# Where a sliding window's mask is applied: selections on POOL, or small products added in PSUM

## The chip, the cores and the metric

The kernel runs on one core of a Trainium2 chip. A core has five engines that run their own instruction queues in order and meet through semaphores: PE (TensorE, the matrix products), DVE (VectorE), ACT (ScalarE), POOL (GpSimd) and SP (SyncE, which here issues nearly all DMAs). PE writes to PSUM alone; DVE and ACT read PSUM, POOL doesn't. The metric is the device time of one execution in microseconds, lower is better.

## The reference, cut to what matters

```
x = A_x                                            # [1, 2048, 512]
g = sigmoid((x * gate_w).sum(-1, keepdims=True))
a = x @ dft_hid_re.T ; b = x @ dft_hid_im.T
A = dft_seq_re @ a - dft_seq_im @ b                # Fourier mixing

qkv = (x @ wqkv) -> q, k, v of 32 heads, 16 wide   # attention
scores = q @ k.T * 16 ** -0.5
mask = (i - j >= 0) & (i - j < 256)                # a sliding window of 256
p = softmax(where(mask, scores, -1e9))
B = (p @ v) @ wo
out = g * A + (1 - g) * B
```

## The kernel before, in words

**Precision.** Most products are made of three: a number is split into a high part of the type float32r (`hi_of`, by ACT) and the rest (`lo_of`, line 104, by DVE or, with `pool`, by POOL), and high x high, high x low and low x high are added up.

**Attention** goes through 8 groups of 4 heads with 16 blocks of 128 positions each, 128 steps in all (the loop at line 942). A step n issues, for each of 4 heads:
- `s_head` (line 404): S = scores of block n's 128 queries against up to 384 keys (line 417). DVE adds the mask, a bf16 tile with 1e30 outside of the window, and takes the row minimum of the negated scores (line 420). Minima of four steps are gathered; `m_rows` and `m_turn` (lines 424 and 430) split them into two parts, turn them with a DVE transposition, write them to DRAM (`m_scr`) and read them back as two further rows of `ring[0]`, so that a later product subtracts the maximum by itself.
- `t_head` (line 465), for the step nine behind (k = n - 9): T = the scores transposed, 128 keys against up to 384 queries, less the maxima (line 475), of which ACT takes the exponential into the tile `pt` (line 476). S uses one half of PE's rows and T the other half, so that both can be in the array at once.

T has no mask. After the four heads of a step, `t_mask` (line 478), deferred by three ticks, has POOL set `pt` to zero in the first 128 columns where the query is ahead of the key, and in the last 128 columns where it is 256 or more behind it: two `affine_select` over 128 x 4 x 128 numbers (lines 482 and 486). In the last two blocks of a group the second is left out.

Every four steps `pv` (line 489) multiplies `pt` by the values, for a block of 512 queries: 88 products (fewer for the first block of a group) of 64 rows and 32 columns of weights, into two banks, one for each half of the keys. A half of 64 keys is taken with 320 columns from its own first, so that the 64 columns ahead of it and behind are never read; for the first key block of a group the ones ahead are read. ACT copies one bank, DVE adds the other (lines 507 and 508), and the result goes to DRAM, where the row of sums is taken out and inverted (`o_pack`, `l_in`, `l_inv`, `l_back`).

**Banks.** S, T and the two outputs of `pv` take turns in four PSUM banks (`ps_a`): an S waits for DVE to be done with the bank two S before, a T for ACT.

**Dense work** is a Python generator, `dense` (line 675): projections to q and k (`qk_proj`), then the Fourier part (`ab_group`, lines 360 to 389, which adds and subtracts four row blocks, and `c_block`, the products along the sequence). `fill` (line 922) takes a fixed number of its products for each step and puts them behind S and T on PE: 1.55 per head while projections last, 2.3 later. Each is a pair, one for each half of the rows.

**Order.** Everything but this is put in place by `defer(ticks, fn)`, a list of due times in ticks (line 83); `tick` is called once per dense product and with 0.7 per head. So a step is about nine ticks, and each engine's queue is the order in which these calls fall due. The input matrices are compared with each other on the way (`check_next`, `compare`), which is work of POOL and ACT.

Results are evicted by `collect` and `evict_split` (line 264): ACT copies, DVE adds the other bank, ACT takes the high part, and DVE or POOL the low one (`qk_evict`, line 281, asks POOL for k and DVE for q). `split_raw` (line 112) splits a loaded weight in two halves; `pool` says how many of its low parts go to POOL.

Of the kernel before, what the change touches and what calls it, by code (L numbers as in the profile page):

```python
# [8 lines left out]
F32 = mybir.dt.float32  # L9
F32R = mybir.dt.float32r  # L10
BF16 = mybir.dt.bfloat16
# [11 lines left out]
NH = 4  # L23
NB = S // P
WIN = 384
BIG = 1e30
SCALE = 0.25
LAG = 9
# [23 lines left out]
def fnet_window_mix(ctx: ExitStack, tc: tile.TileContext, xT, x, wqk, wv, wm, wx, cc, wo, gw, out):  # L52
# [45 lines left out]
    def f(ap):  # L98
        return ap.bitcast(F32)
# [42 lines left out]
    def pt_tile(shape, dt=F32):  # L142
        return at.tile(shape, dt, name="pt", tag="pt", bufs=NPT)

    mask = const.tile([P, WIN], BF16, name="mask")
    T = [const.tile([P, U_W], F32, name=f"t{j}") for j in range(4)]
    nc.gpsimd.memset(T[0], 0.0)
    ps = ps_a.tile([P, 512], F32, name="t", tag="st")
# [39 lines left out]
    for h in range(2):  # L188
        nc.gpsimd.memset(f(ring[1][64 * h + 32:64 * h + 64]), -1.0)

    nc.gpsimd.affine_select(mask, mask, pattern=[[1, WIN]], compare_op=OP.is_gt, fill=BIG,
                            base=0, channel_multiplier=-1)
    nc.gpsimd.affine_select(mask, mask, pattern=[[-1, WIN]], compare_op=OP.is_ge, fill=BIG,
                            base=256, channel_multiplier=1)
    vpad = [const.tile([P, 4, NH, 32], F32, name=f"vpad{b}") for b in range(3)]
    for t in vpad:
        nc.gpsimd.memset(t, 1.0)
# [49 lines left out]
        tick()  # L247

    def es_tile():
        return ev.tile([P, U_W], F32, name="es", bufs=3)  # L250

    def collect(pss, then, scale=1.0):
        t = pt_tile([P, 512]) if len(pss) == 1 else es_tile()[:, 0:512]
# [20 lines left out]
    def qk_evict(g, ss, i, pss):  # L274
        hl = ev.tile([P, 2, 512], F32R, name="hl", bufs=4)

        def done():
            ld(qk_scr[i][g][ss].rearrange("a h p d l s -> (a h p d) l s"), f(hl[:]))
            if i:
                have.add(("qk", g, ss))  # L280
        evict_split(pss, hl[:, 1 - i], hl[:, i], (-SCALE, 1.0)[i], done, i == 1)

    def qk_first(w):
        accs = [acc() for _ in range(2)]
# [75 lines left out]
    def ab_group(q, w, beside):  # L360
        x = [ev.tile([P, U_W], F32, name="ev") for _ in range(3)]
        E, O = slice(0, H + 1), slice(H, 2 * H + 1)
        to = [slice(0, H + 1), slice(H + 1, 2 * H + 2)]

        def t0():
            pass

        def t2():
            minus(x[0], T[0], T[2], False)
            defer(2, plus, T[0], T[0], T[2])  # L370

# [32 lines left out]
    def s_head(n, j):  # L404
        p, h = divmod(j, 2)
        jb = n % NB
        u, jj = divmod(n - LAG, 4)
        if u not in ML:
            ML[u] = at.tile([P, 16], F32, name="nm")
            if not (0 <= LAG + 4 * u and LAG + 4 * u + 4 <= NS * NB):  # L410
                nc.vector.memset(ML[u], 0.0)
        c = (h * 2 + p) * 4 + jj
        k0 = max(0, (jb - 2) * P)
        w = (jb + 1) * P - k0
        r = slice(64 * h, 64 * h + 48)
        ps = ps_a.tile([P, 512], F32, name="s", tag="st")
        nc.tensor.matmul(ps[:, :w], ring[0][r, p, jb * P:(jb + 1) * P], ring[1][r, p, k0:k0 + w],  # L417
                         start=True, stop=True)
        sm = at.tile([P, WIN], BF16, name="sm", bufs=1)
        nc.vector.tensor_tensor_reduce(out=sm[:, :w], in0=ps[:, :w], in1=mask[:, WIN - w:],  # L420
                                       scale=1.0, scalar=3e38, op0=OP.add, op1=OP.min,
                                       accum_out=ML[u][:, c:c + 1])

# [4 lines left out]
        defer(1, m_turn, u, m, hl)  # L428

    def m_turn(u, m, hl):  # L430
        nc.vector.tensor_sub(hl[:, 1], m, f(hl[:, 0]))  # L431
# [33 lines left out]
    def t_head(n, j):  # L465
        p, h = divmod(j, 2)
        kb = n % NB
        q0 = kb * P
        w = min(WIN, S - q0)
        if n not in PT:  # L470
            PT[n] = pt_tile([P, NH, WIN])
        pt = PT[n]
        r = slice(64 * h, 64 * h + 50)
        ps = ps_a.tile([P, 512], F32, name="t", tag="st")
        nc.tensor.matmul(ps[:, :w], ring[1][r, p, q0:q0 + P], ring[0][r, p, q0:q0 + w], start=True, stop=True)  # L475
        nc.scalar.activation(pt[:, j, :w], ps[:, :w], AF.Exp, scale=-1.0)  # L476

    def t_mask(n):
        w = min(WIN, S - n % NB * P)
        pt = PT[n]  # L480
        a = pt[:, :, 0:P]
        nc.gpsimd.affine_select(a, a, pattern=[[0, 4], [1, P]], compare_op=OP.is_ge, fill=0.0,  # L482
                                base=0, channel_multiplier=-1)
        if w == WIN:
            a = pt[:, :, 2 * P:3 * P]
            nc.gpsimd.affine_select(a, a, pattern=[[0, 4], [-1, P]], compare_op=OP.is_gt, fill=0.0,  # L486
                                    base=0, channel_multiplier=1)

    def pv(u, last=False):
        g, sb = divmod(u, 4)  # L490
# [2 lines left out]
        for kb in kbs:  # L493
            pt = PT[g * NB + kb]
            v2 = V2[g * 4 + kb // 4][:, kb % 4]
            for j in range(NH):
                for h in range(2):
                    r = slice(64 * h, 64 * h + 64)
                    a = max(kb * P + (64 * h if kb else 0), sb * 512)
                    e = min(kb * P + 64 * h + 320, sb * 512 + 512)  # L500
                    nc.tensor.matmul(ot[h][32 * j:32 * j + 32, a - sb * 512:e - sb * 512], v2[r, j],  # L501
                                     pt[r, j, a - kb * P:e - kb * P], start=kb == kbs[0], stop=kb == kbs[-1],
                                     skip_group_check=True)
# [4 lines left out]
        defer(3, lambda: nc.vector.tensor_add(os, ot[1], os))  # L508
        hf = g // 4
        us, ls = u_scr[sb][hf], l_scr[sb][hf]  # L510
        d = 14 if hf else 40

        def o_out():
            ld(us[g % 4].rearrange("j r s -> (j r) s"), os)
# [7 lines left out]
            defer(d, l_in)  # L522

        def l_in():
            lt = at.tile([P, 64], F32, name="lt", bufs=2)
            ld(lt, ls[0].rearrange("j (a b) -> (j a) b", b=64))
            defer(d, l_inv, lt)

# [146 lines left out]
    def dense():  # L675
# [9 lines left out]
        for ss in range(4):  # L685
            if ss:
                yield from qk_proj(0, ss, wq0)
            for c in range(4):
                if ss < 3 and c in (1, 2):
                    for a in range(2):  # L690
                        split_x(ss + 1, 2 * c - 2 + a, 1 + 4 * a)
                    if ss < 2:
                        defer(9, load_x, ss + 2, c - 1)
                if ss == 3 and c == 0:
                    raw = load_raw(wqk[1])
                if ss == 3 and c == 2:
                    w = split_raw(raw, 1, 3, 1)
                yield from v_proj(ss * 4 + c, wvs)
        for g in range(1, NG):
            for ss in range(4):  # L700
# [29 lines left out]
            if g < 3:  # L730
                for q in (2 * g - 2, 2 * g - 1):
# [5 lines left out]
                    if q % 2 == 0:  # L737
                        wraw[:] = [load_raw(wqk[g + 1])]
                    else:
                        nextw = split_raw(wraw[0], 1, 3, 1)  # L740
                    yield from ab_group(q, ws, beside)
                w = nextw
        have.add("proj")
# [198 lines left out]
    for n in range(N + LAG + 1):  # L942
# [4 lines left out]
        for p in range(NH):  # L947
# [163 lines left out]
```

## Time and profile before

| what | value |
| --- | --- |
| median of 3 runs | 736.88 us (731.63 to 739.27) |
| the profiled execution | 736.22 us |
| its span | 734.5 us |
| granted TensorE clock | 0.877 of full |
| busy PE / DVE / ACT / POOL | 605.2 / 485.2 / 430.0 / 438.6 us |
| chain that ended last | PE 42%, DMA 15%, DVE 14%, ACT 10%, POOL 7%, issue 7% |

The span is the profiler's, from the first instruction to the last. "Busy" is the time in which an engine has at least one record open; PE's records are pipelined, and their ends are modelled, so PE's busy time says more than its need. A row of the groups names line, engine and operation, output and inputs, shapes, how often, then the busy time in us, the mean length of one in ns, and the idle time just before them with what ended it. A row of waits reads "engine, tile, line <- what it waited for: us in total, times, longest". PEld is the loading of weights, SPq the queue of SP.

### The profile page before, as it was taken

How to read it: one execution, taken by the hardware profiler on the slowest of the kernel's cores; microseconds unless marked ns; L12 is line 12 of the kernel's file. 1: busy time of each engine (PE TensorE's matmuls, PEld its weight loads, DVE VectorE, ACT ScalarE, POOL GpSimd, SP SyncE). 2: the span in 40 equal slices, each digit the busy share in tenths (PEclk: the TensorE clock that was granted, in tenths of full speed). 3: DMA queues.
4: the chain of work that ended last, by engine and by line, in shares of the span. 5: the costliest groups of instructions: out<-in, count | busy, mean ns of one | idle time of the engine just before them, and what ended most of it. 6: DMA issues, size and time to landing. Idle time of an engine off the chain costs nothing.

```text
span 734.5 us, 17636 instructions
## 1 busy us (share of the span) xinstructions
PE 605.2 (82%) x6222; PEld 451.9 (62%) x6222; DVE 485.2 (66%) x1386; ACT 430.0 (59%) x985; POOL 438.6 (60%) x521
## 2 busy tenths in 40 slices
PE   9999799789788888998897778757778889559785
PEld 6788567555464765655565557646666666437554
DVE  5278676877787667787864666685577687344561
ACT  6344577667555667665564757656656777662220
POOL 6022565756676756579684887988997865320000
PEclk9999998999889899999987997767867899858899
DMA  7868777776564766875768778855737774655783
GB/s 287 278 210 239 224 203 223 221 231 201 146 207 135 224 189 209 254 218 167 212 204 268 244 226 280 262 146 192 214 89 211 238 183 124 186 172 152 241 275 129
DMA packets 93606, 152.62 MB, mean 208 GB/s; under 512 B 33028, under 2 KB 42116, under 8 KB 93380
## 3 DMA queue, kind: packets, MB, share of 16 engines
q1 hardware_dynamic: 92068, 149.28, 66.8%
q10 hardware_dynamic: 1440, 2.10, 0.8%
q8 instruction: 53, 0.87, 0.6%
q14 instruction: 45, 0.37, 0.2%
HBM read 108.56 MB, written 47.24 MB: 212 GB/s over the span
## 4 chain that ended last, share of the span: by engine, by line
PE 42%; DMA 15%; DVE 14%; ACT 10%; POOL 7%; issue 7%; SPq 3%; DVEq 0%; ACTq 0%; POOLq 0%
PE d L246 15%; PE o L501 8%; PE s L417 6%; DVE sm L420 6%; PE t L475 6%; PE d L242 4%; DMA ring<-m_scr 3%; DVE mhl L431 3%; SPq L96 3%; ACT pt L476 3%; DMA raw<-cc 3%; ACT cv L543 3%; PE t L242 2%; DMA big<-o_scr 2%; DVE es L508 2%
## 5 line engine op out<-in xcount | busy, mean ns | idle before, releaser
L420 DVE CUSTOM_DVE_ANT_0 sm<-s,mask 128x384 bf16<-128x384 f32 (+2 forms) x512 | 271.2, 530 | 105.1 <-PE s L417 56.8
L476 ACT ACTIVATE pt<-t 128x384 f32<-128x384 f32 (+2 forms) x512 | 231.2, 474 | 110.9 <-PE t L475 85.0
L475 PE MATMUL t<-ring,ring 50*128 50x384 f32 (+2 forms) x512 | 218.8, 442 | 61.9 <-ACT pt L476 23.3
L246 PE MATMUL d<-big,hl 64*128 64x512 f32 (+2 forms) x1440 | 254.0, 387 | 0.6 <-DVE es L257 0.6
L417 PE MATMUL s<-ring,ring 48*128 48x384 f32 (+2 forms) x512 | 200.3, 403 | 34.3 <-DVE nm L420 29.1
L246 PEld LDWEIGHTS d<-big,hl 64*128 64x128 f32 x1440 | 183.1, 225 | 6.5 <-issue 1.9
L482 POOL TENSOR_SCALAR_AFFINE_SELECT pt<-pt 128x512 f32<-128x512 f32 x128 | 85.7, 670 | 140.7 <-ACT pt L476 136.6
L417 PEld LDWEIGHTS s<-ring,ring 48*128 48x128 f32 x512 | 107.4, 214 | 101.0 <-DVE nm L420 86.8
L475 PEld LDWEIGHTS t<-ring,ring 50*128 50x128 f32 x512 | 108.7, 215 | 95.7 <-ACT pt L476 47.6
L246 PE MATMUL d<-hl,big 64*128 64x512 f32 x600 | 111.7, 416 | 0.0
L501 PE MATMUL o<-pt,vpad 64*32 64x320 f32 (+5 forms) x2816 | 88.2, 389 | 13.9 <-POOL pt L482 11.3
L501 PEld LDWEIGHTS o<-pt,vpad 64*32 64x32 f32 x2816 | 68.4, 116 | 36.1 <-POOL pt L482 13.8
L339 POOL TENSOR_TENSOR cv<-cv 128x256 f32<-128x256 f32 (+1 forms) x64 | 75.2, 1175 | 15.8 <-DMA cv<-cc 15.7
L486 POOL TENSOR_SCALAR_AFFINE_SELECT pt<-pt 128x512 f32<-128x512 f32 x112 | 75.8, 677 | 0.0
L246 PEld LDWEIGHTS d<-hl,big 64*128 64x128 f32 x600 | 66.8, 195 | 4.8 <-issue 1.0
L342 POOL TENSOR_TENSOR cv<-cv 128x512 f32<-128x512 f32 x48 | 63.1, 1315 | 8.9 <-DMA cv<-cc 8.9
L507 ACT COPY es<-o 128x512 f32<-128x512 f32 x32 | 18.7, 586 | 78.3 <-PE o L501 76.1
L543 ACT ACTIVATE cv<-cv 128x768 f32<-128x768 f32 x72 | 60.6, 842 | 0.6 <-POOL cv L339 0.6
L508 DVE TENSOR_TENSOR es<-o,es 128x512 f32<-128x512 f32 x32 | 22.1, 691 | 53.3 <-ACT es L507 38.3
L105 POOL TENSOR_TENSOR hl<-raw,hl 128x512 fp32r<-128x512 f32 x35 | 46.0, 1327 | 2.4 <-ACT hl L102 2.4
L242 PE MATMUL t<-big 128*128 128x512 f32 x144 | 39.6, 435 | 9.1 <-DVE fin L896 9.1
L105 POOL TENSOR_TENSOR hl<-es,hl 128x512 fp32r<-128x512 f32 x14 | 18.1, 1290 | 46.1 <-ACT hl L102 45.6
(98 smaller groups left out, 639.2 us busy)
## 6 DMA issues: line engine op xcount, KB each, us to landing
cv<-cc SPq DMA_DIRECT2D x64, 512.0 KB
qk_scr<-hl SPq DMA_DIRECT2D x32, 512.0 KB
ring<-qk_scr SPq DMA_DIRECT2D x128, 128.0 KB
ring<-qk_scr SPq DMA_DIRECT2D x128, 64.0 KB
u_scr<-es SPq DMA_DIRECT2D x32, 256.0 KB
raw<-cc SPq DMA_DIRECT2D x16, 512.0 KB
fin<-r_scr SPq DMA_DIRECT2D x17, 256.0 KB
big<-c_scr SPq DMA_DIRECT2D x16, 258.0 KB
```

What stands on the lines that cost most here:

```text
L105: (nc.gpsimd if pool else nc.vector).tensor_sub(lo, raw, f(hi))
L242: nc.tensor.matmul(pss[0], w, x, start=start, stop=stop, skip_group_check=skip)
L246: nc.tensor.matmul(pss[h], w[r], x[r], start=start, stop=stop, skip_group_check=skip)
L339: (nc.gpsimd if pool else nc.vector).tensor_sub(out, a, b)
L417: nc.tensor.matmul(ps[:, :w], ring[0][r, p, jb * P:(jb + 1) * P], ring[1][r, p, k0:k0 + w], start=True, stop=True)
L420: nc.vector.tensor_tensor_reduce(out=sm[:, :w], in0=ps[:, :w], in1=mask[:, WIN - w:], scale=1.0, scalar=3e38, op0=OP.add, op1=OP.min, accu ...
L475: nc.tensor.matmul(ps[:, :w], ring[1][r, p, q0:q0 + P], ring[0][r, p, q0:q0 + w], start=True, stop=True)
L476: nc.scalar.activation(pt[:, j, :w], ps[:, :w], AF.Exp, scale=-1.0)
L482: nc.gpsimd.affine_select(a, a, pattern=[[0, 4], [1, P]], compare_op=OP.is_ge, fill=0.0, base=0, channel_multiplier=-1)
L486: nc.gpsimd.affine_select(a, a, pattern=[[0, 4], [-1, P]], compare_op=OP.is_gt, fill=0.0, base=0, channel_multiplier=1)
L501: nc.tensor.matmul(ot[h][32 * j:32 * j + 32, a - sb * 512:e - sb * 512], v2[r, j], pt[r, j, a - kb * P:e - kb * P], start=kb == kbs[0], st ...
L543: nc.scalar.activation(junk, src, AF.Abs, accum_out=dst)
```

## The change

T is masked on its bank, ahead of the exponential. The mask is the one that DVE adds to S; its two triangles of 64 x 64 are copied at the start for each half of the rows into `edge`, and `unit` holds two identities. After T's product, two products per head of `unit` (64 x 64, bf16) with `edge` (64 rows, twice 64 columns, or 64 in the last two blocks) add 1e30 to the elements outside of the window: one for keys 0 to 63 and one for keys 64 to 127, into columns 0 to 127 and 256 to 383 in steps. The exponential then gives zero. `t_mask` goes. As the 64 columns ahead of the second half of keys aren't masked, `pv` no longer reads them in the first block either, and the addition there starts at column 64.

Some work is moved from DVE to POOL: the low part of the maxima in `m_turn` (the transposition follows two ticks later, in `m_out`), of q in `qk_evict`, of the second half of three weights (`split_raw` with 2), and two subtractions of `ab_group`. The tiles `es` are 512 columns instead of 516, `lt` has one buffer instead of two, and a delay ahead of `o_pack`, `l_in` and `l_inv` is 30 ticks instead of 40.

```diff
-    mask = const.tile([P, WIN], BF16, name="mask")
+    mask = const.tile([P, MASK_W], BF16, name="mask")
+    edge = const.tile([P, 2, 64], BF16, name="edge")
+    unit = const.tile([P, 64], BF16, name="unit")
...
+    for a in range(2):
+        r = slice(64 * a, 64 * a + 64)
+        for e in range(2):
+            c = 64 * a + 256 * e + 1
+            nc.gpsimd.tensor_copy(edge[r, e], mask[r, c:c + 64])
+    ones = ev.tile([P, U_W], F32, name="ev")[:, 0:P]
+    nc.gpsimd.memset(ones, 1.0)
+    for m in (1, -1):
+        nc.gpsimd.affine_select(ones, ones, pattern=[[m, P]], compare_op=OP.is_ge, fill=0.0,
+                                base=0, channel_multiplier=-m)
+    for a in range(2):
+        r = slice(64 * a, 64 * a + 64)
+        nc.gpsimd.tensor_copy(unit[r], ones[r, r])
...
-        evict_split(pss, hl[:, 1 - i], hl[:, i], (-SCALE, 1.0)[i], done, i == 1)
+        evict_split(pss, hl[:, 1 - i], hl[:, i], (-SCALE, 1.0)[i], done)
...
-            minus(x[0], T[0], T[2], False)
+            minus(x[0], T[0], T[2])
...
-            minus(T[2], T[1], T[3], False)
+            minus(T[2], T[1], T[3])
...
     def m_turn(u, m, hl):
-        nc.vector.tensor_sub(hl[:, 1], m, f(hl[:, 0]))
+        minus(hl[:, 1], m, f(hl[:, 0]))
+        defer(2, m_out, u, hl)
+
+    def m_out(u, hl):
         mt = at.tile([P, 32], F32, name="mt", bufs=1)
...
-        nc.tensor.matmul(ps[:, :w], ring[1][r, p, q0:q0 + P], ring[0][r, p, q0:q0 + w], start=True, stop=True)
+        nc.tensor.matmul(ps[:, :w], ring[1][r, p, q0:q0 + P], ring[0][r, p, q0:q0 + w], start=True, stop=False,
+                         skip_group_check=True)
+        ends = ps.rearrange("p (e c) -> p e c", e=2)
+        d = slice(64 * h, 64 * h + 64)
+        e = 2 if w == WIN else 1
+        for a in range(2):
+            o = slice(64 * a, 64 * a + 64)
+            nc.tensor.matmul(ends[o, 0:e, o], unit[d], edge[d, 0:e], start=False, stop=True, skip_group_check=True)
         nc.scalar.activation(pt[:, j, :w], ps[:, :w], AF.Exp, scale=-1.0)
-
-    def t_mask(n):
...
-                    a = max(kb * P + (64 * h if kb else 0), sb * 512)
+                    a = max(kb * P + 64 * h, sb * 512)
...
-        defer(3, lambda: nc.vector.tensor_add(os, ot[1], os))
+        c = slice(0 if sb else 64, 512)
+        defer(3, lambda: nc.vector.tensor_add(os[:, c], ot[1][:, c], os[:, c]))
...
-        d = 14 if hf else 40
+        d = 14 if hf else 30
...
-                    w = split_raw(raw, 1, 3, 1)
+                    w = split_raw(raw, 1, 3, 2)
...
-            if p == 3 and 0 <= k < N:
-                defer(3, t_mask, k)
```

More of the change, by code (lines that the diff above doesn't have):

```diff
@@ L25 @@
 WIN = 384
+MASK_W = 386
 BIG = 1e30
@@ L189, in fnet_window_mix @@
         nc.gpsimd.memset(f(ring[1][64 * h + 32:64 * h + 64]), -1.0)
-    nc.gpsimd.affine_select(mask, mask, pattern=[[1, WIN]], compare_op=OP.is_gt, fill=BIG,
+    nc.gpsimd.affine_select(mask, mask, pattern=[[1, MASK_W]], compare_op=OP.is_gt, fill=BIG,
                             base=0, channel_multiplier=-1)
-    nc.gpsimd.affine_select(mask, mask, pattern=[[-1, WIN]], compare_op=OP.is_ge, fill=BIG,
+    nc.gpsimd.affine_select(mask, mask, pattern=[[-1, MASK_W]], compare_op=OP.is_ge, fill=BIG,
                             base=256, channel_multiplier=1)
+    for a in range(2):
[11 more added lines that the diff above has]
+        nc.gpsimd.tensor_copy(unit[r], ones[r, r])
     vpad = [const.tile([P, 4, NH, 32], F32, name=f"vpad{b}") for b in range(3)]
@@ L249, in es_tile @@
     def es_tile():
-        return ev.tile([P, U_W], F32, name="es", bufs=3)
+        return ev.tile([P, D], F32, name="es", bufs=3)
     def collect(pss, then, scale=1.0):
@@ L419, in s_head @@
         sm = at.tile([P, WIN], BF16, name="sm", bufs=1)
-        nc.vector.tensor_tensor_reduce(out=sm[:, :w], in0=ps[:, :w], in1=mask[:, WIN - w:],
+        nc.vector.tensor_tensor_reduce(out=sm[:, :w], in0=ps[:, :w], in1=mask[:, WIN - w:WIN],
                                        scale=1.0, scalar=3e38, op0=OP.add, op1=OP.min,
@@ L474, in t_head @@
         ps = ps_a.tile([P, 512], F32, name="t", tag="st")
-        nc.tensor.matmul(ps[:, :w], ring[1][r, p, q0:q0 + P], ring[0][r, p, q0:q0 + w], start=True, stop=True)
-        nc.scalar.activation(pt[:, j, :w], ps[:, :w], AF.Exp, scale=-1.0)
-    def t_mask(n):
[L479 to L487, printed above, removed]
+        nc.tensor.matmul(ps[:, :w], ring[1][r, p, q0:q0 + P], ring[0][r, p, q0:q0 + w], start=True, stop=False,
[6 more added lines that the diff above has]
+            nc.tensor.matmul(ends[o, 0:e, o], unit[d], edge[d, 0:e], start=False, stop=True, skip_group_check=True)
+        nc.scalar.activation(pt[:, j, :w], ps[:, :w], AF.Exp, scale=-1.0)
     def pv(u, last=False):
@@ L524, in l_in @@
         def l_in():
-            lt = at.tile([P, 64], F32, name="lt", bufs=2)
+            lt = at.tile([P, 64], F32, name="lt", bufs=1)
             ld(lt, ls[0].rearrange("j (a b) -> (j a) b", b=64))
@@ L739, in dense @@
                     else:
-                        nextw = split_raw(wraw[0], 1, 3, 1)
+                        nextw = split_raw(wraw[0], 1, 3, 2)
                     yield from ab_group(q, ws, beside)
```

## The prediction

> **What bounds the kernel now.** I read the page first, then the stage in which T's products run (72 to 665 us), the waits inside it, and single switches of PE's tiles in the timeline. The page's chain, and the stage's row:
>
> ```profile
> PE d L246 15%; PE o L501 8%; PE s L417 6%; DVE sm L420 6%; PE t L475 6%; PE d L242 4%; DMA ring<-m_scr 3%; DVE mhl L431 3%; SPq L96 3%; ACT pt L476 3%; DMA raw<-cc 3%; ACT cv L543 3%; PE t L242 2%; DMA big<-o_scr 2%; DVE es L508 2%
> ```
>
> ```profile
> core 0: us, PE busy (x) PEld busy (x) DVE busy (x) ACT busy (x) POOL busy (x), PEclk, DMA share, GB/s
> 72.00:665.00 593.00, 482.92 (x5549) 355.79 (x5553) 412.13 (x1222) 384.04 (x898) 418.70 (x497) 0.86 0.68 203
> ```
>
> No engine fills the stage, and the chain passes through all of them. PE's 483 us count records that overlap: a record lasts longer than the array needs for it. These rows give PE's own need, the first from a stretch where only dense products run:
>
> ```profile
> 60.32 1.56 PE L246 MATMUL d<-big,hl 64*128 64x512 f32 x12
> ```
>
> ```profile
> L246 PE MATMUL d<-big,hl 64*128 64x512 f32 x576 | 130.5, 452 | 0.0
> L246 PE MATMUL d<-hl,big 64*128 64x512 f32 x431 | 89.9, 425 | 0.0
> L246 PE MATMUL d<-big,hl 64*128 64x258 f32 x576 | 80.6, 328 | 0.0
> L246 PE MATMUL d<-big,hl 64*128 64x256 f32 x192 | 33.3, 367 | 0.0
> ```
>
> ```profile
> 125.27 2.45 PE o L501 x63
> ```
>
> Twelve products (six pairs, one for each half of the rows) take 1.56 us with the last one's tail, about 0.23 us a pair. So the stage's 1007 long dense products need 503 x 0.23 = 116 us, the 768 half as long some 384 x 0.12 = 46, 32 blocks of o some 2.4 each = 77, and 512 pairs of s and t, which run beside each other, 0.17 each (shown below) = 87. Together 326 of 593 us. The rest is waiting, in these groups:
>
> ```profile
> PEld s L417 <- DVE nm L420: 86.8, 179, 4.6
> ...
> PEld t L475 <- ACT pt L476: 47.6, 55, 8.2
> ...
> PE s L417 <- DVE nm L420: 29.1, 41, 4.4
> PE t L475 <- ACT pt L476: 23.3, 26, 4.3
> PE t L475 <- DMA ring<-m_scr: 23.3, 9, 8.0
> ...
> PEld t L475 <- DVE es L508: 17.0, 28, 2.7
> PEld o L501 <- POOL pt L482: 13.8, 6, 5.2
> PEld t L475 <- issue: 13.5, 6, 5.2
> PE o L501 <- POOL pt L482: 11.3, 5, 4.9
> ```
>
> They add up to 266 us: s waits for its bank because DVE is behind (116 us, 220 times), t because ACT is (71 us, 81 times), o for POOL's selections (25 us). The kernel is bound by four engines that take turns in being late, with two banks' depth between them.
>
> **What goes.** POOL loses its selections, and DVE loses several operations to POOL:
>
> ```profile
> L482 POOL TENSOR_SCALAR_AFFINE_SELECT pt<-pt 128x512 f32<-128x512 f32 x128 | 85.7, 670 | 140.7 <-ACT pt L476 136.6 <-DMA cv<-cc 3.1 <-PE s L417 0.6
> L486 POOL TENSOR_SCALAR_AFFINE_SELECT pt<-pt 128x512 f32<-128x512 f32 x112 | 75.8, 677 | 0.0
> L431 DVE TENSOR_TENSOR mhl<-nm,mhl 128x16 fp32r<-128x16 f32 x33 | 40.2, 1219 | 3.8 <-ACT mhl L102 3.7
> L105 DVE TENSOR_TENSOR hl<-es,hl 128x512 fp32r<-128x512 f32 x14 | 13.8, 984 | 2.6 <-ACT hl L102 1.1 <-POOL hl L105 0.8 <-issue 0.6
> L105 POOL TENSOR_TENSOR hl<-es,hl 128x512 fp32r<-128x512 f32 x14 | 18.1, 1290 | 46.1 <-ACT hl L102 45.6
> ```
>
> POOL sheds 85.7 + 75.8 = 161 us and takes 14 low parts (18 us), 8 subtractions of ab_group (about as wide: 8 x 1.29 = 10), 3 halves of a weight split (4) and 33 small subtractions of the maxima. The last have no row on POOL; between 0.04 us (16 of 512 columns of the last row) and the 1.2 us that DVE took, 1 to 40 us, I take 0.3 each = 10, nearer to the first, since they are 16 columns wide. POOL ends near 419 - 161 + 42 = 300 us. DVE sheds 40 + 14 + 8 + 3 = 65 us. On the chain lie these three:
>
> ```profile
> 473.22 12.11 DVE mhl L431
> ...
> 544.07 5.95 DVE mhl L431
> ...
> 562.48 5.12 DVE mhl L431
> ```
>
> A subtraction of 16 columns takes 12.1 us there, while POOL's queue runs without a gap; 23 us are on the chain. Gone, I credit 20 of these 23 us, 20 of the 25 us in which o waits for POOL (the rest will be ACT's exponential), and 13 for the other low parts and subtractions: 53 us at most, and only where PE is still the one that waits.
>
> The Trainium skill (SBUF — State Buffer, Who interferes with whom) says that a VectorE instruction with two SBUF inputs contends with GpSimd's reads for a shared interface; the 12.1 us agree. By that rule the transposition, with one input, is never held so, and all of the 23 us would come off, 3 us more.
>
> The maxima come later by two ticks, about 1 us at 9 ticks a block, and the transposition on DVE now waits for POOL's subtraction. Behind it on DVE stand the next L420, and behind these s on PE. One POOL operation in flight costs up to 1.3 us, so 0 to 43 us in 33 turns against the 40 taken away; I take 5, because two ticks cover most of it and POOL's queue is shorter. What is late next would be t's read of m_scr, 23.3 us of waits now; a slower PE stretches ticks as well, so I leave that term alone. Masks and units are made by some ten small POOL instructions at the start, and POOL then waits for work and T for 72 us:
>
> ```profile
> 20.00:40.00 20.00, 20.00 (x101) 15.56 (x101) 5.82 (x18) 7.17 (x14) 0.00 (x0) 1.00 0.77 258
> ```
>
> That costs nothing. The earlier o_pack (30 ticks) and the single lt buffer move three SP transfers that nobody waits for before the tail: nothing; 64 columns less of o and es for the first block: under 3 us, not counted.
>
> **What comes.** Behind each of 512 t products stand two products of 64 x 64 weights and up to 128 columns, in another tile shape than t (64 x 128) before them and than s or d (64 x 128) behind. The trace has such changes of shape at o (64 x 32):
>
> ```profile
> 106.07 0.67 PE L246 MATMUL d<-big,hl 64*128 64x512 f32 x2
> 106.67 0.34 PE L501 MATMUL o<-pt,vpad 64*32 64x64 f32 x8
> ```
>
> ```profile
> 109.02 0.50 PE L246 MATMUL d<-big,hl 64*128 64x512 f32 x2
> 109.35 0.33 PE L475 MATMUL t<-ring,ring 50*128 50x384 f32 x1
> 109.36 0.28 PE L417 MATMUL s<-ring,ring 48*128 48x256 f32 x1
> 109.48 0.45 PE L246 MATMUL d<-big,hl 64*128 64x512 f32 x2
> ```
>
> ```profile
> 109.01 0.18 PEld L246 LDWEIGHTS d<-big,hl 64*128 64x128 f32 x2
> ```
>
> ```profile
> L246 PE MATMUL d<-hl,big x600: 383/393/770, 37.1 to 361.2; 64*128 64x512 f32 x150
> ```
>
> Into o: d's records end at 106.74 and o starts 0.07 us before that, instead of a pair's 0.23 after d's start; so it waits for the array to empty. Out of o: the weights of d are loaded only at 109.01, with d itself, whose record is 0.50 where the median is 0.39 (the second figure of the last row); the load, hidden elsewhere, shows with 0.11. Within one shape t and s start together, and the next d follows 0.13 to 0.17 us later.
>
> For one t then: its record is 0.33, so the small pair starts 0.26 after it. A product of 128 columns lasts 0.22 (t's 384 take 0.33, s's 256 take 0.28, so 128 columns are worth 0.05); weights that show add between nothing and the 0.11 of 128 columns, I take half, 0.06, for 64; the next shape starts 0.07 before the end, at 0.26 + 0.21 = 0.47, and streams after its own 0.11, at 0.58. That is 0.41 us more than 0.17: 512 x 0.41 = 210 us of PE's time. The bounds: 0.06 if the pair needs nothing but its 128 columns (31 us), 0.25 if the array empties but loads stay hidden (128), 0.50 if both loads show fully (256). I take 0.41, as o's switches show both parts each time.
>
> The Trainium skill (TensorEngine Tiling (Array Packing), Key Properties) says that changing the tiling mode, and not just the tile, drains TensorE, and lists 64 x 64 as a mode of its own; o's switch agrees, but no run here shows 64 x 64.
>
> **The sum.** PE's need in the stage goes from 326 to 536 of 593 us. Of the 210 us, what falls where PE waits anyway is free. The 220 waits for DVE, 81 for ACT, 28 for es and 26 others of the rows are 355, about 300 of the 512 cycles once those that coincide count once, and each hides at most 0.41: 120 us. So 90 remain. The waits left, 266 - 120 = 146 us, shrink by what was taken from DVE and POOL, 53, and grow by 5: 90 - 53 + 5 = +42 us on the profiled execution's own 736.2 us. That is 778; the exponentials' start 0.2 us later is inside the 0.41. Against this, a slower PE leaves DVE and ACT more time for each block than the count of waits shows, some 8 us: **770 us**. The profiled execution lies 0.7 us under the median of the runs, which changes nothing.
>
> **The rivals.** *Small products are free of switches* (not slower, in fact faster): where the pair costs 0.06 us, 31 us, half of it inside waits, and the 53 us come off: 736 + 15 - 53 = 698. For it: s, t and d of different row halves do start together (109.35 and 109.36). Against it: every o block. It decides at less than about 0.2 us a pair. Chance 0.22. The Trainium skill (TensorE: Matmul & The Clock Gate, Part 3: Packing small matmuls) lets weight loads overlap products of another row group, without a word on shapes; that is this rival's mechanism, and by it the time would be this rival's.
> *Emptied, but absorbed*: 0.25 us a pair, 128 us; the same 300 waits hide 75, and DVE's shorter queue is given to PE: 128 - 75 - 53 = 0: 736. For it: PE waits 266 us. Chance 0.18.
> *PE sets the pace and ACT lags*: 0.50 us a pair, 256 us, and only the 220 + 81 long waits hide 0.45 of it at best two times in three: 256 - 90 - 53 = +113, cut by the 30 us of waits that cannot recur: about 820. For it: PE is in order, and a late t holds s and d. Chance 0.10.
> Of the change not doing what it says I see no sign: the selections are gone from the program.
>
> **How the numbers follow.** Forecast 0.50, rivals 0.22, 0.18 and 0.10. A measurement of this kernel tells about 1% from no change. Slower by over 1%: 0.50 + 0.10 less a little of the first = 0.59; the middle case spreads on both sides: within 1% 0.12; faster 0.29. The range leaves out half of each far case: 698 to 818; the forecast's own is 748 to 795.
>
> **What would show it.** Right: the two small products start 0.2 us or more behind t, the next product's weights load only with it; exponentials wait longer for PE; no DVE operation of 5 us in the stage; POOL near 300 us; waits of s for DVE well under 116 us; PE busy over 90% of the stage. Wrong: the small pair starts inside t's record beside s or d, PE's share is unchanged, and the stage is shorter than 593 us; or the maxima's transposition waits for POOL by microseconds.

## The result, and the profile after

The changed kernel took 815.36 us (median of 4 runs, 809.81 to 834.97) beside 734.25 us (731.24 to 739.27) for the kernel before: 1.107 times as long, 95% interval 1.094 to 1.121. The profiled one of these four runs was a slow one (span 833.2 us, clock 0.817); the ratios leave such runs out, the medians don't, and the lines below are those of a repetition: span 820.1 us, clock 0.835, median of its two runs 822.8, ratio 1.118 (1.100 to 1.137).

From its page the span, the engines' busy times, the granted clock (in tenths of full, for each fortieth of the span), and the chain:

```profile
span 820.1 us, 19406 instructions
PE 763.9 (93%) x7246; PEld 487.9 (59%) x7246; DVE 422.8 (52%) x1328; ACT 439.7 (54%) x985; POOL 327.6 (40%) x348
PEclk9999699999759599999595879665959599667999
PE 66%; DMA 12%; POOL 7%; issue 5%; DVE 3%; ACT 3%; SPq 3%; POOLq 0%; DVEq 0%; ACTq 0%
PE d L262 31%; PE o L516 9%; PE t L501 9%; PE t L494 7%; PE s L433 5%; PE d L258 4%; SPq L97 3%; DMA ring<-qk_scr 3%; PE t L258 2%; DMA fin<-r_scr 2%; DMA big<-o_scr 2%; DMA ring<-m_scr 2%; DMA qk_scr<-hl 1%; POOL hl L106 1%; POOL t L358 1%
```

PE has gone from 42% of the chain to 66%, DVE from 14% to 3%, and the small products (`PE t L501`) alone hold 9%. The stage of T, which was 593 us long, is now 680; its columns are those of the row in the prediction:

```profile
72.00:752.00 680.00, 642.80 (x6581) 392.89 (x6586) 351.54 (x1172) 394.08 (x898) 300.31 (x311) 0.81 0.60 178
```

PE is busy in 642.80 of 680 us (95%, before 81%). POOL stands at 300.31, DVE fell from 412 to 351.54. Three of the page's groups, and of the waits of the whole execution those that matter:

```profile
L502 ACT ACTIVATE pt<-t 128x384 f32<-128x384 f32 (+2 forms) x512 | 236.6, 471 | 186.7 <-PE t L501 183.2
...
L433 PE MATMUL s<-ring,ring 48*128 48x384 f32 (+2 forms) x512 | 184.0, 368 | 2.0 <-DVE nm L436 1.7
...
L501 PEld LDWEIGHTS <-unit 64*64 64x64 bf16 x1024 | 57.5, 109 | 154.0 <-issue 152.5
```

```profile
DVE sm L436 <- PE s L433: 178.2, 305, 4.5
PEld L501 <- issue: 152.5, 498, 0.5
...
POOL mhl L355 <- ACT mhl L103: 95.4, 19, 21.9
...
DVE mt L452 <- POOL mhl L355: 32.1, 14, 7.4
```

The waits have turned round. S's products hardly wait for DVE any more (1.7 us, before 29.1); DVE waits for S (178.2 us, before 56.8) and ACT for the small products (183.2 us; for T before, 85.0). The row of `PEld L501` is the new one: 498 times the loading of the small weights stands 0.31 us on average, with nothing that the profile names to release it (it calls that "issue"). One such place in the timeline, first PE's products, then the weight loads:

```profile
199.94 0.34 PE L494 MATMUL t<-ring,ring 50*128 50x384 f32 x1
200.21 0.24 PE L501 MATMUL t<-edge,unit 64*64 64x128 bf16 x2
200.38 0.50 PE L262 MATMUL d<-hl,big 64*128 64x512 f32 x2
```

```profile
200.21 0.11 PEld L501 LDWEIGHTS <-unit 64*64 64x64 bf16 x2 [0.31 <-issue]
200.38 0.19 PEld L262 LDWEIGHTS d<-hl,big 64*128 64x128 f32 x2
```

The small pair starts 0.27 us behind T, 0.07 before the end of T's record, and its weights load only then; the next dense pair follows 0.17 later and its record is 0.50 instead of 0.39, with its own weights in the open. The Trainium skill (TensorEngine Tiling (Array Packing), Key Properties) says that a change of the tiling mode drains TensorE. This trace agrees for 64 x 64: the pair starts no earlier than 0.07 us before the end of T's record.

### The profile page after: what moved, and what is told of

Its sections match the earlier page's. It is cut to its first block, busy times and chain, and to the rows that moved or that the text cites. A ratio compares the mean times of both kernels' runs of the same rounds, so it can differ in the third digit from the quotient of the medians.

```text
span 833.2 us, 19406 instructions
## 1 busy us (share of the span) xinstructions
PE 778.2 (93%) x7246; PEld 495.3 (59%) x7246; DVE 423.5 (51%) x1328; ACT 439.9 (53%) x985; POOL 326.7 (39%) x348
## 4 chain that ended last, share of the span: by engine, by line
PE 63%; DMA 14%; POOL 7%; issue 5%; DVE 4%; ACT 3%; SPq 2%; DVEq 0%; POOLq 0%
PE d L262 30%; PE o L516 9%; PE t L501 8%; PE t L494 6%; PE s L433 4%; PE d L258 4%; DMA ring<-m_scr 3%; SPq L97 2%; DMA ring<-qk_scr 2%; DMA big<-o_scr 2%; PE t L258 2%; DVE es L524 1%; POOL hl L106 1%; POOL t L358 1%; POOL t L355 1%
## 5 line engine op out<-in xcount | busy, mean ns | idle before, releaser
L262 PE MATMUL d<-big,hl 64*128 64x512 f32 (+2 forms) x1440 | 264.6, 448 | 0.7 <-DVE es L273 0.7
L494 PE MATMUL t<-ring,ring 50*128 50x384 f32 (+2 forms) x512 | 206.6, 403 | 31.6 <-DVE es L524 13.9
L433 PE MATMUL s<-ring,ring 48*128 48x384 f32 (+2 forms) x512 | 187.4, 374 | 1.8 <-DVE nm L436 1.7
L262 PEld LDWEIGHTS d<-big,hl 64*128 64x128 f32 x1440 | 135.9, 223 | 33.2 <-issue 1.5
L501 PEld LDWEIGHTS <-unit 64*64 64x64 bf16 x1024 | 58.0, 110 | 158.6 <-issue 157.3
L501 PE MATMUL t<-edge,unit 64*64 64x128 bf16 (+1 forms) x1024 | 134.2, 259 | 0.0
L262 PE MATMUL d<-hl,big 64*128 64x512 f32 x600 | 124.9, 490 | 0.0
L516 PE MATMUL o<-pt,vpad 64*32 64x320 f32 (+4 forms) x2816 | 98.1, 429 | 1.1 <-ACT pt L502 0.8
L106 POOL TENSOR_TENSOR hl<-es,hl 128x512 fp32r<-128x512 f32 x28 | 36.4, 1300 | 124.9 <-ACT hl L103 124.2
L524 DVE TENSOR_TENSOR es<-o,es 128x512 f32<-128x512 f32 (+1 forms) x32 | 21.5, 671 | 83.5 <-ACT es L522 72.0
```

The costliest lines, as they stand in the source:

```text
L106: (nc.gpsimd if pool else nc.vector).tensor_sub(lo, raw, f(hi))
L262: nc.tensor.matmul(pss[h], w[r], x[r], start=start, stop=stop, skip_group_check=skip)
L501: nc.tensor.matmul(ends[o, 0:e, o], unit[d], edge[d, 0:e], start=False, stop=True, skip_group_check=True)
```

## The experiments

Four of them part the change into its pieces; the others follow what these left open. Ratios are to runs of the kernel before on the same chip; its medians were 734 to 741 us on the chips used, so differences between the medians of two experiments are good to some us only.

**1. The same masks in T's own shape.** The weights of the small products get 128 columns, an identity with zeros beside it, so that their tile is 64 x 128 like that of T, S and the dense products. The triangles are read straight from the mask.

```diff
-    unit = const.tile([P, 64], BF16, name="unit")
+    unit = const.tile([P, 192], BF16, name="unit")
...
-            nc.tensor.matmul(ends[o, 0:e, o], unit[d], edge[d, 0:e], start=False, stop=True, skip_group_check=True)
+            edge = mask[d, 64 * h + 1:64 * h + 321].rearrange("p (e c) -> p e c", c=64)[:, 0:4 * e - 3:4]
+            nc.tensor.matmul(ends[:, 0:e, o], unit[d, 64 - 64 * a:192 - 64 * a], edge, start=False, stop=True,
+                             skip_group_check=True)
```

> The changed kernel, but each of the two small products has 128 columns of weights (an identity beside a zero block), so that it has T's own tile shape, 64 x 128; it writes all 128 keys, adding zero to one half. The triangles are read straight from the mask tile. Switch theory (the time goes into two changes of tile shape behind each T, with the array emptied and the next weights loaded in the open, and into the lower granted clock that comes with it): 690 to 725 us, granted clock 0.86 or more, the product after a small one starts within 0.15 us of it. Rival (the time goes into 1024 more products and weight loads as such, and into the later start of the exponentials): 790 to 830 us, since here the same number of products has twice the columns.

Measured: 735.2 us (725.56 to 741.45), ratio 0.993 (0.987 to 1.000). The timeline of a place like the one above:

```profile
199.27 0.34 PE L489 MATMUL t<-ring,ring 50*128 50x384 f32 x1
...
199.45 0.23 PE L497 MATMUL t<-mask,unit 64*128 64x128 bf16 x1
199.46 0.40 PE L257 MATMUL d<-hl,big 64*128 64x512 f32 x1
199.52 0.22 PE L497 MATMUL t<-mask,unit 64*128 64x128 bf16 x1
```

The small product starts inside T's record, 0.18 us behind its start, and a dense product of the other half of the rows starts 0.01 us later, between the two small ones, with the usual record of 0.40. The number of products is the changed kernel's, and 80 us are gone (815 against 735). The switch of shape is what the masks cost. (The theory had 690 to 725 us; it left out what the moves cost.)

**2. The moved work alone.** The kernel before, selections and all, with only the work that goes from DVE to POOL.

```diff
-        evict_split(pss, hl[:, 1 - i], hl[:, i], (-SCALE, 1.0)[i], done, i == 1)
+        evict_split(pss, hl[:, 1 - i], hl[:, i], (-SCALE, 1.0)[i], done)
...
-        nc.vector.tensor_sub(hl[:, 1], m, f(hl[:, 0]))
+        minus(hl[:, 1], m, f(hl[:, 0]))
+        defer(2, m_out, u, hl)
```

> The kernel before with its selections on POOL, and only the moved work of the change: low part of the maxima with the later transposition, of q, of the second half of three weights, and two subtractions of ab_group, on POOL. Switch theory: 715 to 740 us, as DVE loses 65 us and its long waits of 5 to 12 us, while POOL gets fuller by some 40 us. Rival (the moves, above all the later maxima, cost a good part of the 80 us): 760 us or more.

Measured: 753.12 us (749.68 to 756.48), ratio 1.027 (1.020 to 1.035). Its chain, and five rows of its waits:

```profile
PE 35%; POOL 21%; DMA 19%; ACT 8%; DVE 7%; issue 6%; SPq 4%; DVEq 0%; POOLq 0%; ACTq 0%
```

```profile
DVE mt L436 <- POOL mhl L339: 70.0, 17, 8.7
...
POOL mhl L339 <- ACT mhl L102: 35.2, 8, 26.8
...
PE t L478 <- DMA ring<-m_scr: 31.9, 15, 4.3
...
PEld o L504 <- POOL pt L485: 23.1, 10, 4.2
...
PE o L504 <- POOL pt L485: 19.5, 8, 3.8
```

The long subtractions on DVE are gone, and in their place DVE's transposition waits for POOL, 17 times and up to 8.7 us. The longest of these waits, on POOL:

```profile
196.79 1.28 POOL L342 TENSOR_TENSOR t<-t,t 128x516 f32<-128x516 f32 x1
...
204.18 1.32 POOL L342 TENSOR_TENSOR ev<-ev,t 128x258 f32<-128x258 f32 x2
205.47 0.21 POOL L339 TENSOR_TENSOR mhl<-nm,mhl 128x16 fp32r<-128x16 f32 x1
```

ACT has the high part ready at 196.78, and POOL does ten other operations without a gap before the subtraction of 0.21 us. The other waits are like it: of the 70.0 us, 65 lie between ACT's end and the start of the subtraction, and POOL works through all of them. (Only 0.4 us are a wait for the high part itself, so POOL's own 35.2 us of waiting for ACT are hardly what holds the transposition.) POOL's share of the chain rises from 7% to 21%. T waits 31.9 us for the maxima, before 23.3, and o waits 42.6 us for the selections on the fuller POOL, before 25.1. The time lies between the two forecasts.

**3. The masks alone.** The changed kernel with all of the moves undone.

```diff
-        minus(hl[:, 1], m, f(hl[:, 0]))
-        defer(2, m_out, u, hl)
+        nc.vector.tensor_sub(hl[:, 1], m, f(hl[:, 0]))
...
-                    w = split_raw(raw, 1, 3, 2)
+                    w = split_raw(raw, 1, 3, 1)
```

> The changed kernel without the moves: small products for the mask, but low parts and subtractions on DVE as before. Switch theory: 810 to 845 us, the same as the changed kernel or somewhat above. Rival (the moves cost): 780 us or less.

Measured: 787.45 us (778.54 to 789.19), ratio 1.076 (1.070 to 1.083). The masks are the larger part of the loss, the moves another 28 us here; this time too lies between the two forecasts. One row of its maxima, with the count and the shortest, middle and longest in ns:

```profile
L447 DVE TENSOR_TENSOR mhl<-nm,mhl x33: 164/250/1429, 40.4 to 668.2; 128x16 fp32r<-128x16 f32 x33
```

The subtractions are on DVE as in the kernel before, but with the selections gone none takes over 1.43 us, where the longest took 12.1; all 33 take 13.8 us instead of 40.2. (In experiments 5 and 6 they are on DVE too, and take 16 to 17 us, none over 1.84.)

**4. No masks at all.** The changed kernel, moves included, with neither selections nor small products.

```diff
-        for a in range(2):
-            o = slice(64 * a, 64 * a + 64)
-            nc.tensor.matmul(ends[o, 0:e, o], unit[d], edge[d, 0:e], start=False, stop=True, skip_group_check=True)
```

> The changed kernel without the small products and without selections: the two ends of the window are not masked at all, so this leaves out a part of the computation. It is the floor for any way of masking. Both theories: 670 to 705 us, granted clock 0.86 or more; the difference from the changed kernel is the whole price of the small products, 110 to 145 us, the difference from the kernel before that of the selections less the moves. If it is above 730, the moves cost more than the selections did.

Measured: 728.05 us (723.86 to 734.28), ratio 0.995 (0.990 to 0.999). So, in medians: the moves +19 (734 to 753), the selections' end -25 (753 to 728, with the small changes that are not moves), the small products +87 (728 to 815). Both theories had priced the small products higher, at 110 to 145 us. The small products of experiment 1 cost at most 7 of these 87 us, and its interval overlaps with this one's.

**5. The same shape, without the moves.** Experiment 1 with the moves undone as in experiment 3; run twice.

> Small products in T's own tile shape, and none of the moved work: low parts and subtractions on DVE as in the kernel before, no selections on POOL. Theory (a change of shape costs about 80 us, the moves about 20, and POOL's selections cost the kernel before some 20): 700 to 720 us, faster than the kernel before by 2 to 4.5%. Rival (the moves cost only where small products or selections crowd the queues): 728 to 742, as with the moves.

> The small products in T's shape without the moves once more. Theory: 707 to 722 us, 2 to 4% faster than the kernel before; DVE's transposition of the maxima waits for nothing on POOL.

Measured: 717.44 us (706.94 to 723.92), ratio 0.966 (0.958 to 0.974), and again 718.12 (710.31 to 722.95), ratio 0.978 (0.964 to 0.993). This beats both kernels, and it is 18 us below the same kernel with the moves: they lose time without the selections too. From the repetition's page and its stage of T:

```profile
span 708.5 us, 19446 instructions
PE 619.2 (87%) x7246; PEld 492.2 (69%) x7246; DVE 454.0 (64%) x1386; ACT 430.2 (61%) x985; POOL 291.4 (41%) x287
PEclk9999999999999999999998998988899899759898
```

```profile
72.00:640.00 568.00, 499.29 (x6577) 397.36 (x6581) 380.73 (x1222) 384.18 (x898) 269.48 (x257) 0.92 0.72 213
```

With 7246 products, as many as in the changed kernel, PE is busy 145 us less. DVE has 29 us more to do in the stage than in the changed kernel (380.73 against 351.54), and the stage is 112 us shorter: how much DVE has to do was not the limit.

**6. The same shape, all moves but the maxima's.** Experiment 1 with `m_turn` as before.

> Small products in T's own tile shape with the moved work on POOL, but for the maxima, whose low part and transposition are on DVE as before. If the maxima's wait is what the moves cost (DVE's transposition stands behind POOL's queue): 705 to 722 us, as without moves. If the other moves cost, above all ab_group's and q's: 728 to 740.

Measured: 726.24 us (724.82 to 729.06), ratio 0.985 (0.978 to 0.992). That lies between experiments 1 (0.993) and 5 (0.966 and 0.978). On the chip of this run the interval is apart from that of experiment 5 (0.958 to 0.974), so the other moves cost something by themselves; from experiment 1 (0.987 to 1.000) it is not apart, so that the maxima's move costs anything here isn't shown. How much each costs stays open.

**7. Half the products, as many switches.** Experiment 3 with one of the two small products behind each T (`range(1)` for `range(2)`).

> Small products of 64 x 64 without the moves, but only one of the two behind each T, so that the ends of the window are left unmasked for half of the keys. Switch theory: the shape changes as often, so 775 to 795 us, as with both (787). Rival (the number of products and weight loads costs): halfway to 734, 755 to 765.

**8. As many products, half the switches.** Experiment 3 with the small products of two heads together behind the second T, and both exponentials after them.

```diff
+        LATE.append((ends, d, e, pt, j, ps, w))
+        if len(LATE) < 2:
+            return
+        for ends, d, e, pt, j, ps, w in LATE:
+            for a in range(2):
...
+        for ends, d, e, pt, j, ps, w in LATE:
+            nc.scalar.activation(pt[:, j, :w], ps[:, :w], AF.Exp, scale=-1.0)
+        LATE.clear()
```

> Small products of 64 x 64 without the moves, all of them, but those of two heads stand behind the second head's T, with both exponentials after them: half as many changes of shape, as many products. Switch theory: halfway from 787 to 734, 750 to 770 us, less what the later exponential of the first head costs (up to 15 us more). Rival (number of products, or their place ahead of the exponential): 780 us or more.

Measured: 787.28 us (772.2 to 792.92) for the first, with no run near the rival's 755 to 765, and 754.83 (751.61 to 764.76), ratio 1.024 (1.016 to 1.031), for the second. The waits of the small weights in experiments 3, 7 and 8, in this order:

```profile
PEld L498 <- issue: 139.6, 503, 0.5
```

```profile
PEld L498 <- issue: 138.7, 497, 0.5
```

```profile
PEld L503 <- issue: 61.8, 248, 0.5
```

Half the products leave the wait, and about the time too, as they were; half the switches halve the wait, and of the 70 us between experiments 3 and 5 (787 and 717) 33 come off. The price goes by the switch.

**9. The changed kernel again**; its lines are in the first section.

> The changed kernel once more, for a profile of an undisturbed execution. Theory: 805 to 822 us, granted clock 0.83 to 0.85, in cycles at full clock the small pair 0.26 to 0.28 us behind T and the next product 0.17 behind the pair with its weights shown; in cycles at half clock both longer by more than half. Rival: the low clock of the first profile was chance, and this one has 0.88 as the masks alone had.

Its trace shows what the switches meet. I sorted the times from the start of one T to that of the next by the clock granted in them ("full" under a tenth at half clock, "half" over nine tenths), and the stretches at half clock by where they end (an experiment's number in brackets, one trace each):

```
                      full clock       half clock       mixed         stretches at half clock
                      n    mean us     n    mean us     n   sum us    n   mean us  end in an o block
before               368   1.053      108   1.149      35    77.7    25    6.7      6
no masks (4)         368   1.008      105    .998      38   101.6    26    6.0      9
changed (9)          358   1.096      127   1.487      26    93.7    14   18.5     14
masks alone (3)      410   1.105       85   1.512      16    48.8    11   15.2     11
half products (7)                                                    13   13.7     13
half switches (8)                                                    15   10.5     12
same shape (1)       424   1.053       61   1.217      26    60.1    18    6.1      5
same, no moves (5)   443   1.022       45   1.251      23    55.0    15    5.9      7
```

"In an o block" is 0.3 us or more behind the block's first record and at most 1.2 behind its last; such places make up 18 to 20% of the stage. With a switch behind every T (the rows 9, 3 and 7) the clock, once halved, came back only there. One such stretch of the changed kernel, in windows with the columns of the prediction's row, and its end in the chain:

```profile
215.50:239.40 23.90, 22.45 (x105) 12.20 (x105) 12.45 (x43) 8.70 (x22) 7.79 (x8) 0.50 0.53 148
239.40:243.20 3.80, 3.80 (x84) 2.75 (x86) 0.67 (x3) 0.12 (x2) 2.47 (x4) 0.53 0.02 3
243.20:253.40 10.20, 10.14 (x100) 5.92 (x89) 7.13 (x24) 6.41 (x14) 0.01 (x1) 1.00 0.47 146
```

```profile
239.63 4.10 PE o L516 x62
```

At half clock PE is busy in 22.45 of 23.90 us, and a switch shows in full:

```profile
226.45 0.41 PE L494 MATMUL t<-ring,ring 50*128 50x256 f32 x1
226.90 0.26 PE L501 MATMUL t<-edge,unit 64*64 64x64 bf16 x2
227.09 0.80 PE L262 MATMUL d<-hl,big 64*128 64x512 f32 x2
227.68 0.41 PE L494 MATMUL t<-ring,ring 50*128 50x256 f32 x1
```

The small pair starts 0.45 us behind T, which has only 256 columns here, and the next pair 0.19 later with a record of 0.80.

**10 and 11. Dense products in bunches.** Is it the o block itself that brings the clock back, or any 4 us without a switch? In the part after the projections, the dense pairs of two steps are held back and issued 18 at a time, in experiment 3 and, as the control, in experiment 5.

```diff
         quota += rate / 2
+        if "proj" in have and quota < 18:
+            return
```

> The changed kernel without the moves (787 us), with the dense pairs of the part after the projections held back and issued 18 at a time, about 4 us of products of one shape every two steps, instead of 2.3 behind each head. The order is worse for all engines, so the time itself, 800 to 900 us, judges nothing; the stretches at half clock do. Theory (a halved clock comes back only after some 4 us without a change of shape): in the bunched part these stretches end inside a bunch or an o block, most of them in a bunch, and their mean falls from 15 us to under 10. Rival (something in the o blocks themselves brings it back, their small weights or their lower load): they still end in o blocks nearly always and stay 13 us or longer.

> The same bunching in the kernel with same-shape small products and no moves (717 us), as the control. Theory: its stretches at half clock were short already (6 us) and stay under 8 us; and if the bunches free the other kernel's clock, the two bunched kernels differ by under 50 us instead of 70. Rival (o blocks alone bring the clock back after shape changes): they differ by 70 us or more.

Measured: 797.97 us (788.1 and 807.84) with the switches and 755.68 (755.44 and 755.92) without: 32 to 52 us apart, instead of 70. The two runs with the switches are 20 us apart, so the time says little. One bunch, with the o block behind it, and the windows up to 612.10 and after:

```profile
608.63 4.16 PE L262 MATMUL d<-big,hl 64*128 64x258 f32 x36
612.72 2.42 PE L513 MATMUL o<-pt,vpad 64*32 64x64 f32 x96
```

```profile
595.10:612.10 17.00, 15.96 (x108) 11.47 (x108) 5.73 (x25) 8.84 (x20) 12.06 (x12) 0.51 0.69 195
612.10:619.00 6.90, 6.29 (x122) 4.18 (x120) 2.70 (x9) 4.25 (x10) 5.06 (x5) 0.97 0.38 100
```

The clock comes back at 612.57, which is 3.9 us into the bunch and 0.15 ahead of the o block. Up to the first bunch, 7 of 7 stretches end in o blocks, with a mean of 13.7 us; from there on 10 of 18 end in a bunch (or up to 1.2 us behind it) and 7 in an o block, with a mean of 7.8 (7.2 in the control). Bunches and o blocks together are 52% of that time, so 9 of 18 would fall there by chance. The o block is not special.

But not every 4 us without a switch will do. Three whole bunches of 4.2 us (from 484.06, 552.15 and 596.42) pass in stretches that go on. The clock changes in steps of 3.41 us, and what tells the last step of a stretch from the others is how much of it has no switch: in experiment 9 the last steps of the 14 stretches hold 2.3 us or more of an o block, the other 62 steps at half clock at most 2.2; in experiments 3 and 7 23 of 24 hold 2.2 us or more, the others at most 2.2; in experiment 11 24 of 25 last steps hold 2.4 us or more of o block or bunch, the other 44 at most 2.5. In the three bunches the boundary of a step lies so that neither side has more.

## Why the prediction was right and wrong

The direction was right, and 815 us lies in the range; but the loss is 81 us, and the forecast had 34. By its own steps:

**The durations of the pair on PE: right, at full clock.** Forecast: the small pair 0.26 us behind T, the next product at 0.58; measured 0.27 and, with the weights' 0.11 behind the start at 0.44, 0.55. Forecast as unhidden: 90 us; between the kernels without masks and changed lie 87.

**How the 87 come about was only half seen.** At full clock the switches hide better than the count of waits said: the mean from T to T rises by 0.088 us against the kernel without masks (1.096 and 1.008), 358 x 0.088 = 32 us where 358 x 0.41 = 147 are spent. Between experiment 5's repetition and experiment 3 it is 410 x 0.083 = 34. The rest stands in time at half clock, which the prediction didn't price: its stage row had 0.86 for the clock, and the sum was made of durations at full clock. There PE has hardly a wait left to hide anything in (1.45 of the 23.90 us above). From no masks to changed, 105 x 0.489 = 51 us come from dearer intervals at half clock, and the remaining 15 of the stage's 97 from more of them; without the moves, 45 x 0.261 = 12 and 20 of 66. That the two errors nearly cancel in the term is chance.

**The selections: right in size.** 20 us forecast for o's waits on POOL; 25 measured with the moves in place, where these waits had grown to 42.6 us, and 2.2 to 3.4% of the time (16 to 25 us) without the moves, where the same-shape products came in.

**The moved work: the step that failed.** "Gone, I credit 20 of these 23 us" for the long subtractions of the maxima and "13 for the other low parts and subtractions", less the 5 for the transposition that "now waits for POOL's subtraction", make -28; experiment 2 has +19. That is 47 us, as much as the whole miss (81 - 34); the other terms' errors, -3 for the pairs, -5 for the selections and the 8 us of slack that didn't come, cancel. With small products in place of the selections the moves cost 18 us (same shape) and 28 (64 x 64). Two parts of the step were wrong.

The wait: the step counted one POOL operation in flight, 0 to 43 us in 33 turns, and took 5 "because two ticks cover most of it". In experiment 2 the wait is 70.0 us, above that bound, and in the changed kernel 32.1. What the transposition waits for is POOL's queue in its order: ten operations stood ahead of the subtraction in the longest case. The price of the instruction itself was no part of the error: 33 of them take 7.9 us on POOL in the changed kernel, 10 forecast.

The credit: the long subtractions were put down to the move, but experiment 3 has them on DVE, and they are short once the selections are gone (13.8 us in all, none over 1.43). So in the changed kernel the move had little of the 23 us left to take away.

How the +19 is made up isn't shown. In experiment 2 the transposition waits 70.0 us, but o also waits 17.5 us more for the selections on the fuller POOL, and experiment 6 has the other moves cost time by themselves. In the changed kernel, where PE and not DVE is what is late, the moves still cost 28 us (experiments 3 and 9); the trace with them has 127 of T's intervals at half clock, the one without 85, so some of their price there runs through the clock, and how they bring that about is open.

**The rivals.** *Free of switches*, 698: wrong for 64 x 64, and its mechanism is what experiments 1 and 5 have, in which the small products start inside T's record. *Emptied but absorbed*, 736: nearly so at full clock (32 of 147 us show), wrong at half. *PE sets the pace and ACT lags*, 820: the time came out near it, by another way: PE does set the pace, but ACT waits for PE (183.2 us), and a switch at full clock costs 0.38 to 0.41, not 0.50.

**The signs** that the prediction asked for came with the loss, but for two: the small pair behind T, weights in the open, ACT's longer waits, POOL at 300, S's waits for DVE nearly gone, PE over 90%. DVE still has one operation of 5 us in the stage (5.42 us at 378.74, a product for the gate and none of the maxima), and the transposition waits for POOL by microseconds, which was listed under wrong.

**Left open:** why a switch behind each T, every 1.1 to 1.5 us, keeps the halved clock from coming back (the trace has the grant, not what it goes by); what starts each stretch; and how much of the moves' price is the maxima's.

## What to carry to other kernels

Where small products are put between larger ones, give them the tile shape of their neighbours, if need be by zeros in the weights: here the products were nearly free, and the switches were 70 to 80 us of 735. Work that another engine waits for is not relieved by an emptier engine with an in-order queue; ask what stands ahead of it in that queue, and who stands behind the one that waits. Price a term on PE at the granted clock of its stage too, since a cost that hides at full clock may have nowhere to hide at half.

## What the runs showed of the hardware

A bf16 product between the float32r ones costs no emptying of the array if the shape is the same: it starts 0.18 us into T's record of 0.34 (experiment 1).

The halved clock comes and goes in steps of 3.41 us (stretches of 3.4, 6.8, 10.2 up to 27.3 us), at 0.50 of full. With a switch of shape behind each T the stretches lasted 18.5 us on average (experiment 9) and ended, 14 of 14, in an o block, though PE's records left hardly a gap; with bunches of products in one shape they were shorter (7.8 us after 13.7, experiment 11), and 24 of 25 ended with a step of which 2.4 us or more had no switch. The Trainium skill (TensorE: Matmul & The Clock Gate, Part 1) has the clock at 4/8 or 8/8, freed after sustained work of about 3.4 us. The trace agrees with the two values and with the length of the step; but PE's records cover 22.45 of 23.90 us of a stretch in which the clock stayed halved, so work in that sense didn't free it. What the runs add is that the length of the stretches went by the switches of shape.
